# Gate factors moved into ScalarE's copies of transposes, and weight decoding started on another rhythm, in a fused attention and two-layer kernel

## The chip, the cores and the metric

One core of one Trainium2 chip runs the whole kernel in one launch. The metric is the device time of that launch in microseconds (us); smaller is better. Before the change it is 1038.77 us, the median of 3 runs (1038.48 to 1040.22).

## What is computed

`q`, `k`, `v` are 4 batches x 8 heads x 576 positions x 64. Each head gives a causal softmax attention `local` and a memory read `mem_out = (phi(q) @ M) / (phi(q) . z)`, with `phi(x) = max(x,0) + exp(min(x,0))`. The two are mixed per head:

```
g = 1 / (1 + exp(-beta))            # one number per head
x = g * mem_out + (1 - g) * local
```

The 2304 x 512 result goes through two layers of the same form, `g(x @ w_in) @ w_out` with 2048 hidden channels. The first has `g(h) = h - tanh(h)`, the second a ratio of polynomials of `h`. All four weight matrices arrive as 64-bit floats and are turned into two fp32r parts (high and low) on the chip.

## The kernel before, in words

**Order.** Nothing is scheduled by a tool: every engine executes its instructions in the order in which the program issues them. In the attention stage that order is a hand-made table: each of the 16 head pairs has some 60 named events (`AT`, `OVER`), each with a due time, and a heap issues them in order of time. After attention, plain loops give the order.

**Attention, one pair `n` of heads.** `scores` (L857) writes q.k products into PSUM for units `i` = 0 to 4 (unit 4 holds the 64 tail rows of both heads). `least` (L873, VectorE, DVE below) masks them, writes them to SBUF and takes each row's minimum of the negated scores; for unit 4 two partial minima are combined by a 1-column operation (L879). `expo` (L886, ScalarE, ACT below) exponentiates and sums. `recip` (L895, L898, DVE) gives 1/sum. `scale` (L906, GpSimd, POOL below) multiplies each row by 1/sum and by `1 - g` of its head in one instruction with two scalar operands. `turn` (L925) transposes the scaled probabilities on TensorE (PE below) in seven groups (`TURNS`), and `turned` (L938, ACT) copies each group from PSUM to SBUF. `values` (L974) multiplies by v. Beside this, `norm1` (L795, POOL), `norm2` (L804, L805, L807, DVE) and `norm3` (L812, POOL) form phi divided by phi.z and times `g`; the factor `g` is L807. `phiT` (L822, PE) transposes phi and `phiC` (L829, ACT) copies it out; `memory` (L958) adds phi @ M onto the same PSUM bank as the values. `setup2` (L1285 to L1292) computes `g`, `1 - g` and a copy of `1 - g` laid out for unit 4.

**Weight decoding.** A background list of pieces (class `Background`, L623) advances when `tick()` is called. A piece is loaded (L557, L559), and at consecutive ticks gets an ACT step (L575), two DVE operations (L577, L578), two more (L582, L585), and then either a split into high and low (L595, L597) or a store to DRAM (L611) for later. Up to two pieces are under way at once.

**Layer 1** runs in two passes: chunks 0 to 3 of the hidden channels on tiles of 256 tokens, woven into and after attention (first lines L1049, L1078, L1079, L1084, L1085, L1096), and chunks 4 to 15 on six tiles of 384 tokens. The second pass is the loop at L1451 with 72 steps (12 a tile). At each of its steps `bg.tick()` is called once for tile 0 and twice after it (L1463, L1465); in this pass the 32 pieces of layer 2's weights are decoded and stored. **Layer 2** follows (L1131 to L1189).

Of the kernel before, what the change touches and what calls it, by code (L numbers as in the profile page):

```python
# [10 lines left out]
F32 = mybir.dt.float32  # L11
F32R = mybir.dt.float32r
I64 = mybir.dt.int64
U32 = mybir.dt.uint32
AF = mybir.ActivationFunctionType
ALU = mybir.AluOpType
AX = mybir.AxisListType
PSUM = bass.MemoryType.PSUM

P = 128  # L20
# [7 lines left out]
TURNS = (((2, 0, 3), (0, 0, 1)), ((2, 1, 3), (0, 1, 1)), ((3, 0, 4),), ((3, 1, 4),), ((1, 0, 2), (1, 1, 2)), ((4, 0, 4),), ((4, 1, 1),))  # L28
MIX_FROM = 680.0
BG_FROM = 411.57  # L30
N_PT = 6
AGE_A, AGE_B, AGE_C = 1, 3, 4

AT = {'s1': 48.5,
 's2': -9.21,
# [427 lines left out]
BANKS_1 = ([0, 1], [2, 5], [3], [4], [6, 7])  # L463
# [8 lines left out]
def kernel(  # L472
# [19 lines left out]


    nc = tc.nc
    B, NP, _, _, S = qd.shape
    H, D = 2 * NP, mz.shape[2] // 2
    NT, DM = out.shape
# [70 lines left out]
    def w_decode(layer, f, s):  # L568


        words = wraw.pop((layer, f, s)).bitcast(U32).rearrange("p (c t) -> p c t", t=2)
        low, high = words[:, :, 0], words[:, :, 1]
        x = bg.buf("wf", [P, DM], U32, f"wf{layer}_{f}_{s}")
        xf = x.bitcast(F32)
        nc.scalar.activation(xf, high.bitcast(F32), AF.Abs)  # L575
        yield
        nc.vector.tensor_scalar(xf, xf, E_MIN, E_MAX, ALU.max, ALU.min)  # L577
        nc.vector.tensor_scalar(  # L578
            x, x, 5, 2, ALU.logical_shift_left, ALU.logical_shift_right
        )  # L580
        yield
        nc.vector.scalar_tensor_tensor(  # L582
            x, high, 0xC0000000, x, ALU.bitwise_and, ALU.bitwise_or
        )
        nc.vector.scalar_tensor_tensor(  # L585
            x, low, 29, x, ALU.logical_shift_right, ALU.bitwise_or
        )
        yield
        return xf

# [32 lines left out]
    class Background:  # L623
# [3 lines left out]
        def __init__(self):  # L627
            self.q, self.live, self.nl, self.ns, self.held = [], [], 0, 0, 0
            self.ring = {t: [(stage, t)] * 2 for t in ("wraw", "wf")}
            self.at = {"wraw": 0, "wf": 0}  # L630
            self.now, self.loaded, self.age = 0, [], 1

        def more(self, pool):
            for t in self.ring:
# [6 lines left out]

        def leave(self):

            while self.ns - len(self.live) < self.mark:
                self.tick(self.ns < self.mark)

        def buf(self, tag, shape, dt, name):
# [12 lines left out]
        def tick(self, start=True):  # L660
            self.now += 1
            for item in list(self.live):
                item[0] += 1
                self.held -= item[0] == item[1]
                if next(item[3], self) is self:
                    self.live.remove(item)
            if (
                start and self.ns < self.nl
                and self.now >= self.loaded[self.ns] + self.q[self.ns][4]
                and len(self.live) < len(self.ring["wf"])  # L670
            ):
                _, done, key, work, _ = self.q[self.ns]
                self.ns += 1
                next(work)
                self.live.append([1, done, key, work])
            while self.nl < len(self.q) and self.held < len(self.ring["wraw"]):
                load, _, key, *_ = self.q[self.nl]
                load(*key)
                self.held += 1
                self.loaded.append(self.now)  # L680
                self.nl += 1
# [21 lines left out]
    class Attention:  # L703
# [95 lines left out]

        def norm2(self, n):  # L800

            d, h = self.pair[n], 2 * (n % NP)
            nrm = d["nrm"] = self.sp.tile([P, NQ + 1, 2], F32, tag="nrm", name=f"nrm{n}")
            nc.vector.tensor_reduce(nrm, self.cp["pz"][n % 2], AX.X, ALU.add)  # L804
            nc.vector.reciprocal(nrm, nrm)  # L805
            gg = self.cp["g"][:, h:h + 2].unsqueeze(1)
            nc.vector.tensor_tensor(nrm, nrm, gg.to_broadcast([P, NQ + 1, 2]), ALU.mult)  # L807

        def norm3(self, n):
            d = self.pair[n]  # L810
# [15 lines left out]
        def phiC(self, n, k):  # L826
            d = self.pair[n]
            j0, w = ((0, TB), (TB, TAIL))[k]
            nc.scalar.copy(d["phiT"][:, j0:j0 + w], d.pop(("php", k))[:, 0:w])  # L829


        def scores(self, n, units):
# [29 lines left out]
        def least(self, n, i):  # L862

            v, cp = self.u[n, i], self.cp
            sm = v["sm"]
            for c, (bank, c0, k0, k1, _, mask) in enumerate(v.pop("jobs")):
                if i < NQ:
                    v["p"].append(self.sp.tile(
                        [P, k1], F32, tag=f"p{i}_{c}", name=f"p{n}_{i}_{c}", bufs=1
                    ))  # L870
                elif c == 0:
                    v["p"].append(cp["p4"])
                nc.vector.tensor_tensor_reduce(  # L873
                    out=v["p"][-1][:, k0:k1], in0=bank[:, c0:c0 + k1 - k0], in1=mask,
                    scale=-0.125, scalar=3.0e38, op0=ALU.add, op1=ALU.min,
                    accum_out=sm[:, 4 + c:5 + c],
                )
            if i == NQ:
                nc.vector.tensor_tensor(sm[:, 4:5], sm[:, 4:5], sm[:, 5:6], ALU.min)  # L879

        def expo(self, n, i, e):

            v = self.u[n, i]
            sm, pt = v["sm"], v["p"][e]
            pt = pt[:, 0:S] if i == NQ else pt
            nc.scalar.activation(  # L886
                pt, pt, AF.Exp, bias=sm[:, 4 + e:5 + e], scale=-1.0,
                accum_out=sm[:, 2 * e:2 * e + 1],
            )

# [8 lines left out]

        def scale(self, n, i, e):  # L900
            v, h = self.u[n, i], 2 * (n % NP)
            pt = v["p"][e]
            og, c = (self.cp["omg"], h + e) if i < NQ else (self.cp["omg4"], n % NP)
            pt = pt[:, 0:S] if i == NQ else pt
            eng = nc.vector if (n, i, e) == (0, NQ - 1, 0) else nc.gpsimd
            eng.tensor_scalar(  # L906
                pt, pt, v["sm"][:, 6 + e:7 + e], og[:, c:c + 1], ALU.mult, ALU.mult
            )

        def busy(self, ps, count):  # L910

# [19 lines left out]
        def turned(self, n, k):  # L931
            ps = self.pair[n].pop(("tp", k))
            w = sum(nb for _, _, nb in TURNS[k])
            if w == 1:
                t = self.sp.tile([P, 1, P], F32, tag="pT5", name=f"pT{n}_{k}")
            else:
                t = self.sp.tile([P, NQ, P], F32, tag="pT", name=f"pT{n}_{k}", bufs=N_PT)
            nc.scalar.copy(t[:, 0:w, :].rearrange("r t c -> r (t c)"), ps[:, 0:w * P])  # L938
            c = 0
            for i, e, nb in TURNS[k]:  # L940
                self.u[n, i].setdefault("pT", {})[e] = t[:, c:c + nb]
                c += nb
# [303 lines left out]
    cp["g"] = cpool.tile([P, H], F32, tag="gg", name="gg")  # L1246
    cp["omg"] = cpool.tile([P, H], F32, tag="omg", name="omg")
    cp["omg4"] = cpool.tile([P, NP], F32, tag="omg4", name="omg4")
    cp["sm"] = [cpool.tile([P, 8], F32, tag=f"sm{j}", name=f"sm{j}") for j in range(2 * NQ + 2)]
    cp["rq"] = [cpool.tile([P, S + TAIL], F32, tag=f"rq{j}", name=f"rq{j}") for j in range(2)]  # L1250
    cp["mb"] = [cpool.tile([P, P], F32, tag=f"mb{j}", name=f"mb{j}") for j in range(3)]
# [31 lines left out]
    def setup2():  # L1283
        g, omg = cp["g"], cp["omg"]
        nc.scalar.activation(g, g, AF.Exp, scale=-1.0)  # L1285
        nc.vector.tensor_scalar(g, g, 1.0, None, ALU.add)
        nc.vector.reciprocal(g, g)
        nc.vector.tensor_scalar(omg, g, -1.0, 1.0, ALU.mult, ALU.add)
        o2 = omg.rearrange("r (p e) -> r p e", e=2)
        for e in range(2):  # L1290
            r = slice(e * TAIL, (e + 1) * TAIL)
            nc.vector.tensor_copy(cp["omg4"][r], o2[r, :, e])  # L1292

    bS, bT, bV = (Banks(i) for i in BANKS_0)
    bHa, bYa = (Banks(i) for i in BANKS_1[3:])
# [30 lines left out]
    bg.more(wke)  # L1326
    bg.age = AGE_A
    for f in FA:
        bg.add(1, f, w_direct, f"wa{f}", nc.gpsimd)
    for f in FB[len(FB) - KEEP:]:  # L1330
        bg.add(1, f, w_keep)
    attn.start(setup)
# [22 lines left out]

    while events:
        at, _, name, n = heapq.heappop(events)
        if attn.done and not mixed:
            mixed = True
            bS.ids, bT.ids, bV.ids = BANKS_1[:3]  # L1360
        if name in ("h", "xs") and (not mixed or flow["n"] == len(one.items)):
# [38 lines left out]
    slot_of = {f: f"wb{j}" if j < nb else f"wa{j - nb}" for j, f in enumerate(FB)}  # L1400
    for j, f in enumerate(FB):
        if j < len(FB) - KEEP:
            bg.add(1, f, w_direct, slot_of[f], nc.gpsimd)
    bHa.ids = bHa.ids + BANKS_1[0]
    tiles = list(range(NT // TM))
    two = None
    while any(flow["line"]) or one.out or flow["n"] < len(one.items):
        advance(True, True)
        left = len(one.items) - flow["n"]
        if left == LESS_AT:  # L1410
            bg.less()
        if left == 0 and two is None:
            bg.leave()
            wke_ctx.close()
# [36 lines left out]
    for s in range(ni + 2):  # L1451
# [7 lines left out]
        if s < ni:  # L1459
            two.gate1(t, f)  # L1460
            if s % nf in SPLITS_1 and t + 1 < len(tiles):
                xs1.ready(t + 1, SPLITS_1[s % nf])
            bg.tick()  # L1463
            if t > 0:
                bg.tick()  # L1465
        if s >= 2:
            two.tail(*items[s - 2])
# [97 lines left out]
```

## Time and profile before

| | before |
|---|---|
| median of 3 runs | 1038.77 us |
| the profiled execution, its own time | 1039.35 us |
| its span, first to last instruction | 1037.6 us |
| mean granted TensorE clock | 0.996 |
| PE busy, share of the span | 97% |
| DVE, ACT, POOL busy | 76%, 68%, 35% |

All rows below come from that one profiled execution. A span row gives busy time by engine; a chain row follows the work that ended last, back from the end, so that a piece of it is time that nothing else hid. A matmul's end is modelled, and a busy PE is not a PE at its peak. "issue" in the chain is time in which an engine waited for nothing that the profile shows.

### The profile page before, as it was taken

The page shows a single profiled execution, that of the slowest core. Times are in us where ns is not written, and L with a number is a line of the kernel's source. Part 1 is how long each engine was busy: PE and PEld are TensorE (multiplying, and loading weights), DVE is VectorE, ACT ScalarE, POOL GpSimd, SP SyncE. Part 2 cuts the span into 40 slices and gives each one's busy share as a digit, 9 for nine tenths or more (in the row PEclk, how much of TensorE's full clock was granted, in tenths as well). Part 3 has the DMA queues.
Part 4 walks back from the last instruction along what each step waited for, and adds up shares of the span by engine and source line. Part 5 has one row for each costly group of instructions (what it writes and reads, how often), then busy time and mean ns, then how long its engine had stood idle before and what let it go on. Part 6 is the DMA issues. An engine that isn't in the chain of part 4 may idle for free.

```text
span 1037.6 us, 18004 instructions
## 1 busy us (share of the span) xinstructions
PE 1010.9 (97%) x6446; PEld 912.2 (88%) x6446; DVE 784.7 (76%) x1759; ACT 701.5 (68%) x1492; POOL 362.6 (35%) x380
## 2 busy tenths in 40 slices
PE   7999999999988999999999999999999999999998
PEld 4766777888988999999999999999999999999997
DVE  5889999874878366757676767987877877877885
ACT  5878877785555443333333556998888888888886
POOL 4878896673543010101000101332332423323221
PEclk9999999999999999999999999999999999999999
DMA  4445556432232124444444441000000000000000
GB/s 131 124 148 146 166 133 203 140 109 73 82 103 82 41 92 122 122 128 128 136 126 123 141 144 41 21 1 32 1 11 22 1 31 1 1 31 1 22 10 31
DMA packets 37674, 82.97 MB, mean 80 GB/s; under 512 B 8528, under 2 KB 11088, under 8 KB 37584
## 3 DMA queue, kind: packets, MB, share of 16 engines
q1 hardware_dynamic: 37120, 81.55, 26.1%
q8 instruction: 51, 0.84, 0.3%
q14 instruction: 39, 0.32, 0.1%
q10 hardware_dynamic: 464, 0.27, 0.1%
HBM read 66.07 MB, written 15.73 MB: 79 GB/s over the span
## 4 chain that ended last, share of the span: by engine, by line
PE 80%; DVE 12%; ACT 4%; issue 2%; POOL 1%; DMA 0%; SPq 0%; DVEq 0%; ACTq 0%; POOLq 0%
PE h L1049 35%; PE y L1179 19%; PE y L1096 17%; PE s L857 3%; DVE p L873 3%; PE tp L925 2%; PE pv L974 2%; DVE wf L585 2%; DVE wf L582 1%; ACT p L886 1%; DVE gl L1085 1%; DVE wf L577 1%; DVE phi L789 1%; PE pw L974 1%; DVE wf L578 1%
## 5 line engine op out<-in xcount | busy, mean ns | idle before, releaser
L1049 PE MATMUL h<-xs,w 128*128 128x384 f32 (+1 forms) x2448 | 437.4, 327 | 1.6 <-POOL xs L1041 0.7
L1049 PEld LDWEIGHTS h<-xs,w 128*128 128x128 f32 x2448 | 408.2, 188 | 12.5 <-POOL xs L1041 1.3
L1096 PE MATMUL y<-gh,w 128*128 128x384 f32 (+1 forms) x864 | 216.3, 318 | 3.0 <-ACT gh L1084 2.9
L1179 PE MATMUL y<-w,gh 128*128 128x512 f32 x576 | 179.6, 393 | 0.0
L1096 PEld LDWEIGHTS y<-gh,w 128*128 128x128 f32 x864 | 152.2, 189 | 4.3 <-ACT gh L1084 3.1
L1096 PE MATMUL y<-gl,w 128*128 128x384 f32 (+1 forms) x432 | 137.6, 318 | 4.0 <-DVE gl L1085 3.9
L1041 POOL TENSOR_TENSOR xs<-x,xs 128x256 fp32r<-128x256 f32 (+1 forms) x56 | 51.3, 940 | 256.1 <-ACT xs L1040 232.8
L1078 ACT ACTIVATE g<-h 128x384 f32<-128x384 f32 (+1 forms) x108 | 49.2, 455 | 134.6 <-PE h L1049 121.0
L1079 DVE TENSOR_TENSOR g<-h,g 128x384 f32<-128x384 f32 (+1 forms) x108 | 55.2, 512 | 97.2 <-ACT g L1078 97.0
L906 POOL TENSOR_SCALAR p<-p,sm,omg 128x256 f32<-128x256 f32 (+4 forms) x143 | 109.2, 773 | 48.8 <-DVE sm L898 34.7
L1179 PEld LDWEIGHTS y<-w,gh 128*128 128x128 f32 x576 | 106.8, 188 | 17.4
L1179 PE MATMUL y<-w,gl 128*128 128x512 f32 x288 | 114.0, 396 | 0.2
L1168 POOL TENSOR_TENSOR gl<-g,gh 128x384 fp32r<-128x384 f32 x48 | 49.5, 1031 | 149.8 <-ACT gh L1166 149.8
L1168 POOL TENSOR_TENSOR gl<-vG,gh 128x384 fp32r<-128x384 f32 x47 | 50.3, 1070 | 131.2 <-ACT gh L1166 129.0
L886 ACT ACTIVATE p<-p,sm 128x128 f32<-128x128 f32 (+4 forms) x144 | 84.9, 592 | 12.2 <-DVE sm L873 8.3
L1084 ACT CAST gh<-g 128x384 fp32r<-128x384 f32 (+1 forms) x108 | 51.6, 478 | 61.2 <-PE y L1096 58.6
L1096 PEld LDWEIGHTS y<-gl,w 128*128 128x128 f32 x432 | 81.6, 189 | 5.2 <-DVE gl L1085 5.2
L1155 DVE TENSOR_TENSOR vA<-vA,vC 128x384 f32<-128x384 f32 x96 | 53.5, 558 | 42.9 <-ACT vC L1149 42.9
L873 DVE CUSTOM_DVE_ANT_0 p<-s,mask 128x512 f32<-128x512 f32 (+4 forms) x160 | 69.5, 478 | 17.3 <-PE s L857 15.2
L1085 DVE TENSOR_TENSOR gl<-g,gh 128x384 fp32r<-128x384 f32 (+1 forms) x108 | 61.8, 573 | 23.6 <-ACT gh L1084 23.6
L857 PE MATMUL s<-rk,rq 64*128 64x512 f32 (+5 forms) x320 | 71.9, 475 | 7.8 <-DVE sm L873 5.1
L1144 DVE SCALAR_TENSOR_TENSOR vA<-vA,vC 128x384 f32<-128x384 f32 x96 | 59.3, 618 | 25.2 <-ACT vC L1143 20.1
(95 smaller groups left out, 1607.2 us busy)
## 6 DMA issues: line engine op xcount, KB each, us to landing
wraw<-in_w_in_dram SPq DMA_DIRECT2D x32, 512.0 KB, 4.1
wraw<-in_w_out_dram SPq DMA_DIRECT2D x32, 512.0 KB, 4.0
wk<-wf SPq DMA_DIRECT2D x42, 256.0 KB, 4.4
wx<-wk SPq DMA_DIRECT2D x21, 512.0 KB, 3.3
qn<-in_qn_dram SPq DMA_DIRECT2D x16, 320.0 KB, 3.7
vn<-in_vn_dram SPq DMA_DIRECT2D x16, 320.0 KB, 4.3
out_dram<-o SPq DMA_DIRECT2D x18, 256.0 KB, 2.0
rk<-in_kd_dram SPq DMA_DIRECT2D x30, 144.0 KB, 2.8
```

What stands on the lines that cost most here:

```text
L857: nc.tensor.matmul(bank[:, c0:c0 + k1 - k0], d["rq"][r, q0:q0 + P], d["rk"][r, k0:k1], start=True, stop=True, skip_group_check=True,)
L873: nc.vector.tensor_tensor_reduce(out=v["p"][-1][:, k0:k1], in0=bank[:, c0:c0 + k1 - k0], in1=mask, scale=-0.125, scalar=3.0e38, op0=ALU.ad ...
L886: nc.scalar.activation(pt, pt, AF.Exp, bias=sm[:, 4 + e:5 + e], scale=-1.0, accum_out=sm[:, 2 * e:2 * e + 1],)
L906: eng.tensor_scalar(pt, pt, v["sm"][:, 6 + e:7 + e], og[:, c:c + 1], ALU.mult, ALU.mult)
L1049: nc.tensor.matmul(ps[:, 0:T], wi_of(layer, f, wp, k), xs[k][:, xp], start=(n == 0), stop=(n == 3 * NK - 1),)
L1079: nc.vector.tensor_tensor(v["g"], v["h"], v["g"], ALU.subtract)
L1085: self.lo.tensor_tensor(v["gl"], v["g"], v["gh"].bitcast(F32), ALU.subtract)
L1096: nc.tensor.matmul(ps, wo_of(1, f, w)[:, m * P:(m + 1) * P], v[g], start=(first and j == 0 and m % n == 0), stop=(last and j == 2), skip_g ...
L1144: nc.vector.scalar_tensor_tensor(A, A, QEPS, C, ALU.add, ALU.mult)
L1155: nc.vector.tensor_tensor(n["A"], n["A"], n["C"], ALU.mult)
L1168: eng.tensor_tensor(o["gl"], o["G"], o["gh"].bitcast(F32), ALU.subtract)
L1179: nc.tensor.matmul(acc_of[t][m], g[:, c], wo_of(2, f, w), start=(first and j == 0), stop=(last and j == 2),)
```

## The change

1. **Probabilities.** For units 0, 2 and 3 (`LATE`) POOL multiplies by 1/sum alone, one operation with one scalar operand. The factor `1 - g` is applied in `turned`: the ACT copy of that transpose group becomes an activation `Copy` whose scale is a per-partition operand holding the head's `1 - g`. Groups 0 to 3 of the seven hold those units. Units 1 and 4 stay as they were.
2. **Norm.** L807 goes. `phiC` becomes an activation `Copy` with scale `g` (new tile `g4`, laid out by head pair), filled by two more small copies in `setup2`.
3. **Unit 4's minimum.** L879, a `tensor_tensor` of two 1-column operands, becomes a `tensor_reduce` over those two neighbouring columns into column 7, which `expo` then reads.
4. **Decoding.** A layer 2 piece starts only 3 ticks or more after the last start (`EVERY`), and after tile 0 the number of ticks per step follows a 12-entry list (`TICKS_1`, sum 24) where it was 2 at each step.

The event table, its times and the events' names stay. Other new names (`N_P`, `MIX`, `PSUM_DECODE`, `SCALES`, `ENG`, `LOW_*`, `bg.banks`, `bg.inside`) hold values with which the code does what it did: `PSUM_DECODE` is False, and every engine letter is "P".

```diff
+SCALES = "PPPPPPPPP"
+LATE = (0, 2, 3)
+EVERY = 3
+TICKS_1 = (2, 2, 2, 3, 2, 3, 2, 2, 2, 2, 2, 0)
...
             if (
                 start and self.ns < self.nl
                 and self.now >= self.loaded[self.ns] + self.q[self.ns][4]
+                and (self.q[self.ns][2][0] == 1 or self.now >= self.last + EVERY)
                 and len(self.live) < len(self.ring["wf"])
             ):
                 _, done, key, work, _ = self.q[self.ns]
+                self.last = self.now
...
         def norm2(self, n):
...
             nc.vector.reciprocal(nrm, nrm)
-            gg = self.cp["g"][:, h:h + 2].unsqueeze(1)
-            nc.vector.tensor_tensor(nrm, nrm, gg.to_broadcast([P, NQ + 1, 2]), ALU.mult)
...
         def phiC(self, n, k):
-            nc.scalar.copy(d["phiT"][:, j0:j0 + w], d.pop(("php", k))[:, 0:w])
+            nc.scalar.activation(
+                d["phiT"][:, j0:j0 + w], d.pop(("php", k))[:, 0:w], AF.Copy,
+                scale=self.cp["g4"][:, n % NP:n % NP + 1],
+            )
...
             if i == NQ:
-                nc.vector.tensor_tensor(sm[:, 4:5], sm[:, 4:5], sm[:, 5:6], ALU.min)
+                nc.vector.tensor_reduce(sm[:, 7:8], sm[:, 4:6], AX.X, ALU.min)
...
         def scale(self, n, i, e):
-            eng = nc.vector if (n, i, e) == (0, NQ - 1, 0) else nc.gpsimd
-            eng.tensor_scalar(
-                pt, pt, v["sm"][:, 6 + e:7 + e], og[:, c:c + 1], ALU.mult, ALU.mult
-            )
+            how = "V" if (n, i, e) == (0, NQ - 1, 0) else SCALES[2 * i + e]
+            eng = nc.vector if how == "V" else nc.gpsimd
+            if i == NQ:
+                og = self.cp["omg4"][:, n % NP:n % NP + 1]
+                eng.tensor_scalar(pt[:, 0:S], pt[:, 0:S], r, og, ALU.mult, ALU.mult)
+            elif i not in LATE:
+                og = self.cp["omg"][:, h + e:h + e + 1]
+                eng.tensor_scalar(pt, pt, r, og, ALU.mult, ALU.mult)
+            elif how == "A":
+                nc.scalar.activation(pt, pt, AF.Copy, scale=r)
+            else:
+                eng.tensor_scalar(pt, pt, r, None, ALU.mult)
...
-            nc.scalar.copy(t[:, 0:w, :].rearrange("r t c -> r (t c)"), ps[:, 0:w * P])
+            dst, (i, e, _) = t[:, 0:w, :].rearrange("r t c -> r (t c)"), TURNS[k][0]
+            if i in LATE:
+                c = 2 * (n % NP) + e
+                nc.scalar.activation(
+                    dst, ps[:, 0:w * P], AF.Copy, scale=self.cp["omg"][:, c:c + 1]
+                )
+            else:
+                nc.scalar.copy(dst, ps[:, 0:w * P])
...
         for e in range(2):
             r = slice(e * TAIL, (e + 1) * TAIL)
             nc.vector.tensor_copy(cp["omg4"][r], o2[r, :, e])
+            nc.vector.tensor_copy(cp["g4"][r], g2[r, :, e])
...
-            bg.tick()
-            if t > 0:
+            for _ in range(TICKS_1[s % nf] if t else 1):
                 bg.tick()
```

## Rows read from the trace of the kernel before

**Rows 1.** Busy time by engine in six stretches of the span (us; instructions in brackets).
```profile
core 0: us, PE busy (x) PEld busy (x) DVE busy (x) ACT busy (x) POOL busy (x), PEclk, DMA share, GB/s
...
77.00:125.00 48.00, 44.78 (x385) 32.69 (x383) 44.95 (x146) 39.09 (x106) 41.20 (x44) 0.96 0.49 147
125.00:252.00 127.00, 124.52 (x1174) 101.81 (x1174) 102.99 (x348) 95.21 (x265) 87.75 (x98) 1.00 0.48 142
...
345.00:640.00 295.00, 294.74 (x1699) 294.18 (x1698) 193.18 (x332) 122.58 (x240) 26.42 (x24) 1.00 0.40 118
640.00:1037.60 397.60, 393.13 (x1965) 353.79 (x1964) 319.83 (x576) 338.83 (x608) 119.52 (x115) 1.00 0.04 14
```

**Rows 2.** Chain that ended last, 12 to 28 us: start, us, what.
```profile
12.70 0.16 DVE omg L1292
...
12.87 0.17 DVE omg L1292
...
13.62 0.52 POOL p L906
...
14.34 1.61 POOL p L906 x2
...
16.32 0.94 POOL p L906
...
19.92 0.17 DVE nrm L807
...
21.86 2.46 POOL p L906 x3
```

**Rows 3.** The same chain, 66 to 117 us: pieces of L879 and L807.
```profile
67.83 1.39 DVE sm L879
...
87.63 0.04 DVE nrm L807
87.66 0.27 issue
...
94.79 0.43 DVE sm L879
...
116.52 0.04 DVE nrm L807
116.56 0.26 issue
```

**Rows 4.** Small DVE operations by line: duration ns min/median/max, first and last start.
```profile
L879 DVE TENSOR_TENSOR sm<-sm x16: 159/160/1379, 15.4 to 242.4; 128x1 f32<-128x1 f32 x16
...
L895 DVE TENSOR_REDUCE sm<-sm x80: 135/148/159, 13.1 to 245.4; 128x2 f32<-128x4 f32 x64, 128x1 f32<-128x2 f32 x16
```

**Rows 5.** Groups by shape, DVE: busy us, mean ns.
```profile
L879 DVE TENSOR_TENSOR sm<-sm 128x1 f32<-128x1 f32 x16 | 4.7, 293 | 0.6
...
L807 DVE TENSOR_TENSOR nrm<-nrm,gg 128x10 f32<-128x10 f32 x16 | 3.8, 237 | 0.5
```

**Rows 6.** POOL: L906 by line (ns min/median/max), one of it, one without scalar operands.
```profile
L906 POOL TENSOR_SCALAR p<-p,sm,omg x143: 442/768/1432, 13.6 to 246.0; 128x384 f32<-128x384 f32 x32, 128x128 f32<-128x128 f32 x32, 128x256 f32<-128x256 f32 x32, 128x512 f32<-128x512 f32 x31
...
72.42 0.82 POOL L906 TENSOR_SCALAR p<-p,sm,omg 128x576 f32<-128x576 f32 x1 [0.73 <-ACT p L886]
...
L1266 POOL TENSOR_SCALAR_AFFINE_SELECT mask<-mask 128x128 f32<-128x128 f32 x1 | 0.3, 294 | 0.1
```

**Rows 7.** Groups by shape, ACT, PSUM to SBUF: without and with scale and bias operands.
```profile
L1148 ACT ACTIVATE vA<-h 128x384 f32<-128x384 f32 x96 | 46.9, 489 | 39.4 <-PE h L1049 37.4
...
L1152 ACT ACTIVATE vG<-h,coef 128x384 f32<-128x384 f32 x48 | 31.5, 656 | 0.0
```

**Rows 8.** The chain again: first and last ACT copies on it (L829, L938).
```profile
31.66 0.10 ACT phiT L829
...
54.40 0.59 ACT pT L938
...
214.98 0.10 ACT phiT L829
...
219.12 0.49 ACT pT L938
```

**Rows 9.** Who waited for whom, 0 to 250 us: us in total, times, longest.
```profile
ACT pT L938 <- PE tp L925: 18.6, 25, 2.3
...
PEld tp L925 <- POOL p L906: 12.4, 18, 1.6
...
PE tp L925 <- POOL p L906: 2.7, 4, 1.0
```

**Rows 10.** Waits of 345 to 640 us: PE's only one, and ACT's cast behind PE.
```profile
ACT gh L1084 <- PE y L1096: 56.8, 55, 1.6
...
PE h L1049 <- DVE w L621: 0.3, 1, 0.3
```

**Rows 11.** Groups by shape, DVE: the last two operations of a decode step.
```profile
L585 DVE SCALAR_TENSOR_TENSOR wf<-wraw,wf 128x512 uint32<-128x512 uint32 x64 | 52.8, 824 | 2.2
L582 DVE SCALAR_TENSOR_TENSOR wf<-wraw,wf 128x512 uint32<-128x512 uint32 x64 | 51.9, 811 | 0.6
```

More of the change, by code (lines that the diff above doesn't have):

```diff
@@ L31 @@
 N_PT = 6
+N_P = 1
+MIX = True
+PSUM_DECODE = False
+SCALES = "PPPPPPPPP"
+LATE = (0, 2, 3)
+LOW_ATT, LOW_POST, LOW_X = "P", "P", "P"
 AGE_A, AGE_B, AGE_C = 1, 3, 4
+EVERY = 3
+TICKS_1 = (2, 2, 2, 3, 2, 3, 2, 2, 2, 2, 2, 0)
 AT = {'s1': 48.5,
@@ L494 @@
     nc = tc.nc
+    ENG = {"P": nc.gpsimd, "V": nc.vector}
     B, NP, _, _, S = qd.shape
@@ L572, in w_decode @@
         low, high = words[:, :, 0], words[:, :, 1]
-        x = bg.buf("wf", [P, DM], U32, f"wf{layer}_{f}_{s}")
-        xf = x.bitcast(F32)
+        nm = f"wf{layer}_{f}_{s}"
+        if bg.banks:
+            x = bg.banks(nm + "x").bitcast(U32)
+            bg.inside += 1
+        else:
+            x = bg.buf("wf", [P, DM], U32, nm)
+        inside, xf = bool(bg.banks), x.bitcast(F32)
         nc.scalar.activation(xf, high.bitcast(F32), AF.Abs)
@@ L584, in w_decode @@
         )
+        y = bg.buf("wf", [P, DM], U32, nm) if inside else x
         nc.vector.scalar_tensor_tensor(
-            x, low, 29, x, ALU.logical_shift_right, ALU.bitwise_or
+            y, low, 29, x, ALU.logical_shift_right, ALU.bitwise_or
         )
+        bg.inside -= inside
+        xf = y.bitcast(F32)
         yield
@@ L631, in __init__ @@
             self.now, self.loaded, self.age = 0, [], 1
+            self.banks, self.inside, self.last = None, 0, 0
         def more(self, pool):
@@ L642, in leave @@
         def leave(self):
-            while self.ns - len(self.live) < self.mark:
+            while self.ns - len(self.live) < self.mark or self.inside:
                 self.tick(self.ns < self.mark)
@@ L800, in norm2 @@
         def norm2(self, n):
-            d, h = self.pair[n], 2 * (n % NP)
+            d = self.pair[n]
             nrm = d["nrm"] = self.sp.tile([P, NQ + 1, 2], F32, tag="nrm", name=f"nrm{n}")
@@ L868, in least @@
                     v["p"].append(self.sp.tile(
-                        [P, k1], F32, tag=f"p{i}_{c}", name=f"p{n}_{i}_{c}", bufs=1
+                        [P, k1], F32, tag=f"p{i}_{c}", name=f"p{n}_{i}_{c}", bufs=N_P
                     ))
@@ L878, in least @@
             if i == NQ:
-                nc.vector.tensor_tensor(sm[:, 4:5], sm[:, 4:5], sm[:, 5:6], ALU.min)
+                nc.vector.tensor_reduce(sm[:, 7:8], sm[:, 4:6], AX.X, ALU.min)
         def expo(self, n, i, e):
             v = self.u[n, i]
-            sm, pt = v["sm"], v["p"][e]
+            sm, pt, c = v["sm"], v["p"][e], 7 if i == NQ else 4 + e
             pt = pt[:, 0:S] if i == NQ else pt
             nc.scalar.activation(
-                pt, pt, AF.Exp, bias=sm[:, 4 + e:5 + e], scale=-1.0,
+                pt, pt, AF.Exp, bias=sm[:, c:c + 1], scale=-1.0,
                 accum_out=sm[:, 2 * e:2 * e + 1],
@@ L901, in scale @@
             v, h = self.u[n, i], 2 * (n % NP)
-            pt = v["p"][e]
-            og, c = (self.cp["omg"], h + e) if i < NQ else (self.cp["omg4"], n % NP)
-            pt = pt[:, 0:S] if i == NQ else pt
-            eng = nc.vector if (n, i, e) == (0, NQ - 1, 0) else nc.gpsimd
-            eng.tensor_scalar(
-                pt, pt, v["sm"][:, 6 + e:7 + e], og[:, c:c + 1], ALU.mult, ALU.mult
-            )
+            pt, r = v["p"][e], v["sm"][:, 6 + e:7 + e]
+            how = "V" if (n, i, e) == (0, NQ - 1, 0) else SCALES[2 * i + e]
[10 more added lines that the diff above has]
+                eng.tensor_scalar(pt, pt, r, None, ALU.mult)
         def busy(self, ps, count):
@@ L937, in turned @@
                 t = self.sp.tile([P, NQ, P], F32, tag="pT", name=f"pT{n}_{k}", bufs=N_PT)
-            nc.scalar.copy(t[:, 0:w, :].rearrange("r t c -> r (t c)"), ps[:, 0:w * P])
+            dst, (i, e, _) = t[:, 0:w, :].rearrange("r t c -> r (t c)"), TURNS[k][0]
[4 more added lines that the diff above has]
+                )
+            else:
+                nc.scalar.copy(dst, ps[:, 0:w * P])
             c = 0
@@ L1248 @@
     cp["omg4"] = cpool.tile([P, NP], F32, tag="omg4", name="omg4")
+    cp["g4"] = cpool.tile([P, NP], F32, tag="g4", name="g4")
     cp["sm"] = [cpool.tile([P, 8], F32, tag=f"sm{j}", name=f"sm{j}") for j in range(2 * NQ + 2)]
@@ L1288, in setup2 @@
         nc.vector.tensor_scalar(omg, g, -1.0, 1.0, ALU.mult, ALU.add)
-        o2 = omg.rearrange("r (p e) -> r p e", e=2)
+        o2, g2 = (t.rearrange("r (p e) -> r p e", e=2) for t in (omg, g))
         for e in range(2):
@@ L1328 @@
     for f in FA:
-        bg.add(1, f, w_direct, f"wa{f}", nc.gpsimd)
+        bg.add(1, f, w_direct, f"wa{f}", ENG[LOW_ATT])
     for f in FB[len(FB) - KEEP:]:
@@ L1357 @@
         at, _, name, n = heapq.heappop(events)
-        if attn.done and not mixed:
+        if MIX and attn.done and not mixed:
             mixed = True
@@ L1402 @@
         if j < len(FB) - KEEP:
-            bg.add(1, f, w_direct, slot_of[f], nc.gpsimd)
-    bHa.ids = bHa.ids + BANKS_1[0]
+            bg.add(1, f, w_direct, slot_of[f], ENG[LOW_POST])
+    bHa.ids = BANKS_1[3] + BANKS_1[0]
+    if PSUM_DECODE:
+        bg.banks = Banks(BANKS_1[1] + BANKS_1[2])
+    xs_a.eng = ENG[LOW_X]
     tiles = list(range(NT // TM))
@@ L1411 @@
             bg.less()
+        if left <= 2:
+            bg.banks = None
         if left == 0 and two is None:
```

## The prediction

> **What bounds the kernel now.** I read the busy time by stretch first. From 345 us to the end PE is the engine that works without a gap: 294.74 of 295 us, then 393.13 of 397.6 [rows 1]. What can still move lies before that, in attention, where no engine alone sets the pace: from 77 to 125 us DVE is busy 44.95 of 48 us, from 125 to 252 us PE 124.52 of 127 with DVE at 103 and ACT at 95 [rows 1]. So I read the chain that ended last, to see which instructions of this change lie on it. It passes back and forth between PE, DVE and ACT, and touches L807, L879, L906, L829 and L938 in a few places only [rows 2, 3, 8]. Third come the durations of those lines by shape [rows 4 to 7], and last the waits [rows 9, 10].
>
> All engines run in issue order and the order stays, so I count what leaves or joins the chain; time won before 345 us shifts all that follows, since nothing later starts by a clock.
>
> **L879, the unit 4 minimum.** It is on the chain in 7 of 16 pairs, with 0.17, 1.39, 0.20, 0.43, 0.16, 0.16 and 0.16 us, 2.67 in all (the two longest stand in [rows 3]). An undisturbed one takes 159 ns, yet one took 1379 [rows 4]. Its successor is a `tensor_reduce` like L895, which took 135 to 159 ns in all 80 cases among the same neighbours, mean about 148 [rows 4]. 7 x 0.148 = 1.04, so the gain is 1.63 us. The least gain is 7 x 0.012 = 0.08, if whatever held L879 up holds up the next DVE operation instead.
>
> **L807, the factor g in the norm.** It is on the chain in 5 pairs: 0.17 twice in the first pairs [rows 2], 0.04 three times from 87 to 117 us, there followed by 0.27, 0.08 and 0.26 us of "issue" before the next DVE operation starts [rows 3]. Together 0.34 + 0.12 + 0.61 = 1.07 us that go. Without the two long delays (0.27 and 0.26 brought down to 0.08) it is 0.70, the least gain. POOL's norm3 behind it starts earlier; nothing more is counted for that.
>
> **Set-up.** The two L1292 copies are on the chain, 0.16 and 0.17 us [rows 2]. Two more of their kind stand beside them: +0.33 us.
>
> **L906 on POOL, one operand less.** No row shows POOL's single-operand form. The shortest L906, 128 columns, took 442 ns; POOL's pass over 128 columns without scalar operands, the affine select, 294 [rows 6]. Two operands and a second multiply thus cost at most 148 ns, and I take half, 74, for the one that goes; the ends are 0 and 148. Seven L906 lie on the chain, all in the first two pairs [rows 2]: 7 x 0.074 = 0.52 us gained, with ends 0 and 1.04. The other 88 of the 95 POOL instructions in question are hidden: PE waited for L906 in 4 places only, 2.7 us in all, while most of the weight loader's 12.4 us ran beside matmuls [rows 9].
>
> A rule of the Trainium skill speaks against this gain. From 128 columns to 576, L906 goes from 442 to 820 ns, 0.84 ns a column [rows 6]. The GPSIMD Engine Reference, section "Elementwise — side-by-side cycle accounting", says that a loop body of up to two operations is bound by the read and write port at 1.03 cycles an element, 0.86 ns at the 1.2 GHz it gives; the trace agrees. So, by that rule, dropping the second multiply would save nothing per column; by that the sum below would be 1.28 us of gain, and the time 1037.5.
>
> **The scaled ACT copies.** 4 of 7 L938 per pair and both L829 get a scale operand: 64 + 32 = 96 instructions. From PSUM, 128x384 without operands takes 489 ns and with two 656 [rows 7]: (656 - 489) / 2 = 83.5 ns each, some 8.0 us of ACT time. The chain holds 12 pieces of L938, from 54.40 to 219.12 us, and 6 of L829, from 31.66 to 214.98 [rows 8]. 12 x 4/7 is about 7, plus 6 makes 13 x 0.0835 = 1.09 us lost. The ends are 0 (the copy only shortens a wait behind it) and 18 x 0.0835 = 1.50. The rest is covered by ACT's idle time, 32 us from 125 to 252 [rows 1], with ACT itself waiting for the transposes 25 times [rows 9]; if that cover goes, see the second rival.
>
> **Decoding.** I count ticks through the 72 steps of the loop. Before, the 32 layer 2 pieces start at steps 11 to 58; after, at steps 12 to 57, each at most one step away from where it was, eight in a tile both times, and none in a tile's last step. Nothing is left over for the flush at step 60. The DMAs move with them: the last store goes from step 59 to 60, the loads' buffers come free a step earlier at the end, and SP's queue has the same number of entries. In this stretch PE waits once, for 0.3 us, for another line, and ACT's cast waits for PE's matmuls 55 times, not the reverse [rows 10]. So 0, with 0.3 us as the most to win; the price of a collision is the third rival.
>
> **Sum.** -1.63 - 1.07 + 0.33 - 0.52 + 1.09 = -1.80 us, against the profiled execution's own 1039.35: 1037.55. That execution is 0.58 us above the median of 1038.77, so on the median: 1037.0. At the ends: -1.63 - 1.07 + 0.33 - 1.04 = -3.41, 1035.4; and -0.08 - 0.70 + 0.33 + 1.50 = +1.05, 1039.8.
>
> **Rivals.** *DVE's relief counts everywhere.* If DVE's queue set the pace in all 16 pairs, all of L807 (16 x 237 ns = 3.79 us) and the shortening of L879 (16 x 145 = 2.32) would show [rows 5]: -6.11 + 0.33 - 0.52 + 1.09 = -5.21, 1033.6 us. For it: DVE is 94% busy from 77 to 125 us [rows 1], and freed DVE time may also relieve collisions with POOL that I don't see. Against it: the chain holds only 7 and 5 of the 16.
>
> *ACT becomes the bound.* If ACT's copies hold up its exponentials, and these the transposes of the next turn, the whole 8.02 us shows: -1.63 - 1.07 + 0.33 - 0.52 + 8.02 = +5.13, 1043.9 us. It makes the kernel measurably slower once some 60 of the 96 copies are on the path, (2.08 + 2.89) / 0.0835, against 13 now. For it: ACT is 81% busy from 77 to 125 us and the chain passes through it repeatedly up to 219 us. Against it: the idle time above.
>
> *A decode step lands in front of a gate.* L582 and L585 take 0.81 + 0.82 us [rows 11]. If such a pair now stood once per tile in front of a gate that PE needs at once, four tiles would cost 4 x 1.64 = 6.5 us beside the gain: 1043.5 us. DVE's 102 us of idle time in that stretch [rows 1] speak against it.
>
> **How the numbers follow.** The measurement tells 0.2%, 2.08 us, from no change: faster is under 1036.7, slower above 1040.8. My own sum has a chance of 0.58; its ends reach over the line, so 0.16 of that is faster and 0.42 within. Wide DVE relief has 0.24 (faster). ACT as the bound has 0.12 (slower) and decode collisions 0.06, half of it slower, half within. Faster 0.16 + 0.24 = 0.40; within 0.42 + 0.03 = 0.45; slower 0.12 + 0.03 = 0.15. The likeliest is the own sum, 1037.0, alone 1035.4 to 1039.8. The range reaches to the first rival, 1033.6, and a little past it for lucky collisions, 1033.0; at the top past the sum's end to 1040.5, leaving out the two slow rivals and a rest below: 0.2.
>
> **What would show it.** The new minimum at 135 to 160 ns in all 16 cases; L906's 128-column minimum near 368 ns, with units 1 and 4 unchanged; L938 and L829 longer by some 84 ns in the scaled groups; attention ending 1 to 3 us earlier and the same shift standing at 345 us and at the end; PE still without a gap from 345 to 640. Wrong would be: single-operand POOL instructions at the old duration or longer, DVE's long delays moved to its neighbours, ACT without idle time before its exponentials, or any time won or lost after 345 us.

## The result, and the profile after

The changed kernel takes **1051.76 us**, the median of 4 runs (1050.76 to 1052.73), beside 1039.35 us for the kernel before (4 runs, the three of the section above among them). The ratio is 1.0119, 95% interval [1.0102, 1.0137]: 12.4 us slower, where 1.8 us faster was forecast and 1040.5 us was the top of the range.

Where the time went by stretch, as in [rows 1]:

```profile
core 0: us, PE busy (x) PEld busy (x) DVE busy (x) ACT busy (x) POOL busy (x), PEclk, DMA share, GB/s
...
77.00:125.00 48.00, 42.29 (x370) 30.68 (x371) 41.20 (x134) 39.34 (x106) 47.90 (x42) 0.96 0.47 133
125.00:252.00 127.00, 122.00 (x1122) 97.32 (x1121) 108.63 (x351) 96.75 (x259) 112.49 (x101) 1.00 0.45 135
...
345.00:640.00 295.00, 294.74 (x1701) 294.42 (x1700) 187.08 (x329) 119.44 (x239) 25.71 (x25) 1.00 0.40 119
```

From 77 to 125 us POOL is busy 47.90 of 48 us; before it was 41.20, and DVE, then at 44.95, has fallen to 41.20. From 125 to 252 us POOL went from 87.75 to 112.49, though attention no longer ends within this stretch. From 345 to 640 us PE is as full as before, 294.74 us.

The last matmuls of attention, in the timeline of PE, before and then after (start, us):

```profile
252.11 0.80 PE L974 MATMUL pw<-pT,vn 128*64 128x64 f32 x20
```

```profile
264.20 0.80 PE L1008 MATMUL pw<-pT,vn 128*64 128x64 f32 x20
```

Attention ends 12.1 us later. The span grew by 11.7 us (1037.6 to 1049.3), so the whole loss lies in attention and is carried on nearly unchanged. It starts early: the 35th of the 112 copies of transposes comes 7.6 us later already (before, then after):

```profile
78.81 0.57 ACT L938 COPY pT<-tp 128x512 f32<-128x512 f32 x1
```

```profile
86.36 0.57 ACT L972 COPY pT<-tp 128x512 f32<-128x512 f32 x1
```

The instructions that changed, in the changed kernel. L935 is the multiply of units 0, 2 and 3 that was L906 (units 1 and 4 are now L931 and L928); the first two lines are its summary and one of 512 columns, the others groups by shape (count | busy us, mean ns):

```profile
L935 POOL TENSOR_SCALAR p<-p,sm x95: 595/1347/2228, 13.9 to 253.7; 128x384 f32<-128x384 f32 x32, 128x128 f32<-128x128 f32 x32, 128x512 f32<-128x512 f32 x31
...
90.06 1.57 POOL L935 TENSOR_SCALAR p<-p,sm 128x512 f32<-128x512 f32 x1
...
L935 POOL TENSOR_SCALAR p<-p,sm 128x512 f32<-128x512 f32 x31 | 53.7, 1734 | 6.3 <-DVE sm L919 4.3 <-ACT gh L1118 2.0
...
L968 ACT ACTIVATE pT<-tp,omg 128x512 f32<-128x512 f32 x64 | 43.4, 687 | 6.3 <-PE tp L952 6.0
...
L972 ACT COPY pT<-tp 128x512 f32<-128x512 f32 x32 | 18.6, 582 | 15.6 <-PE tp L952 15.6
```

The multiply has one operation less and takes far longer. The shortest, 128 columns, is 595 ns where it was 442 [rows 6]. From 128 to 512 columns it goes to 1.57 us, (1570 - 595) / 384 = 2.5 ns a column, where the rows before gave 0.84. ACT's scaled copies take 687 ns against 582 for the plain ones beside them, 105 ns more where 83.5 was forecast.

The chain that ended last, 83 to 101 us, in the changed kernel:

```profile
83.99 0.60 POOL p L935
...
85.96 1.55 POOL p L935 x2
...
87.75 1.10 POOL p L935
88.85 1.23 POOL w L614
90.08 1.54 POOL p L935
...
93.11 1.75 POOL p L935
94.86 0.04 issue
94.90 0.66 PE tp L952 x4
```

The path runs through POOL's queue: L935, what is queued behind it (L614, a weight split), L935 again, and only then PE's transposes. Before, POOL's multiply of all units stood on the chain with seven instructions, all before 25 us [rows 2]; now L935 alone stands there with 26, in 18 pieces that start from 13.92 to 164.08 us. PE waits for L935 directly, 10 times and 8.6 us in all, where it was 4 times and 2.7 us for all units [rows 9]:

```profile
PE tp L952 <- POOL p L935: 8.6, 10, 2.2
```

### The profile page after: what moved, and what is told of

Read it like the earlier page. It is cut to its first block, busy times and chain, and to the rows that moved or that the text cites. A ratio compares the mean times of both kernels' runs of the same rounds, so it can differ in the third digit from the quotient of the medians.

```text
span 1049.3 us, 17994 instructions
## 1 busy us (share of the span) xinstructions
PE 1014.6 (97%) x6446; PEld 912.8 (87%) x6446; DVE 780.0 (74%) x1745; ACT 709.8 (68%) x1492; POOL 404.4 (39%) x380
## 4 chain that ended last, share of the span: by engine, by line
PE 79%; DVE 10%; POOL 5%; ACT 3%; issue 2%; DMA 0%; SPq 0%; DVEq 0%; POOLq 0%; ACTq 0%
PE h L1083 35%; PE y L1213 19%; PE y L1130 17%; POOL p L935 3%; PE s L878 2%; PE tp L952 2%; DVE p L894 2%; PE pv L1008 1%; DVE wf L600 1%; DVE wf L596 1%; DVE gl L1119 1%; DVE wf L591 1%; POOL xs L1075 1%; ACT p L907 1%; PE pv L992 1%
## 5 line engine op out<-in xcount | busy, mean ns | idle before, releaser
L1075 POOL TENSOR_TENSOR xs<-x,xs 128x256 fp32r<-128x256 f32 (+1 forms) x56 | 49.0, 898 | 258.8 <-ACT xs L1074 235.6
L935 POOL TENSOR_SCALAR p<-p,sm 128x128 f32<-128x128 f32 (+2 forms) x95 | 123.5, 1311 | 23.4 <-ACT p L907 12.0
L952 PEld LDWEIGHTS tp<-ident,p 128*128 128x128 f32 x400 | 46.0, 145 | 38.8 <-POOL p L935 15.2
```

The lines of the kernel that those rows point to most:

```text
L935: eng.tensor_scalar(pt, pt, r, None, ALU.mult)
L952: nc.tensor.transpose(ps[:, (c + j) * P:(c + j + 1) * P], p[:, (c1 + j) * P:(c1 + j + 1) * P], self.cp["ident"],)
L1075: self.eng.tensor_tensor(xs[:, 1], src, xs[:, 0].bitcast(F32), ALU.subtract)
```

## The experiments

**Theory A:** GpSimd runs the multiply without a second operation on a slower path, and that alone makes the kernel slower. **Theory B:** one of the other edits does. Small edits of the multiply, and the decode rhythm, tell them apart.

### e1_imm and e2_ones: the second operation put back

```diff
-                eng.tensor_scalar(pt, pt, r, None, ALU.mult)
+                eng.tensor_scalar(pt, pt, r, 1.0, ALU.mult, ALU.mult)               # e1_imm
+                eng.tensor_scalar(pt, pt, r, self.cp["one"], ALU.mult, ALU.mult)    # e2_ones
```

e2_ones also sets up the tile `one`, 128x1, filled with 1.0 once.

> The changed kernel, but GpSimd's multiply for units 0, 2 and 3 keeps two operations: 1/sum as operand, then the constant 1.0. Theory A (the one-operation form runs slowly on GpSimd: 1552 ns at 512 columns in the trace after, 768 before): its floors return to about 770, 660 and 440 ns for 512, 384 and 128 columns, GpSimd's busy time falls by about 40 us, and the time is 1037 +-2 us, what the other edits were forecast to give. Theory B (the added ScalarE operand, the moved norm factor or the decode rhythm lost the 12 us): the time stays at 1049 to 1053 us, whatever GpSimd does.

> As the run before, but the second operand is a per-partition tile of ones, so that the instruction has the very form of the kernel before. Theory A: 1037 +-2 us and L906's old durations. If only the constant's form is slow: this one is fast and the run before is not. Theory B: 1049 to 1053 us.

Measured: **e1_imm 1034.26 us**, ratio to the kernel before 0.9956 [0.9941, 0.9971]; **e2_ones 1037.39 us**, 0.9987 [0.9978, 0.9996]. L935 by line (ns min/median/max), e1_imm and then e2_ones:

```profile
L935 POOL TENSOR_SCALAR p<-p,sm x95: 360/691/1349, 13.6 to 235.8; 128x384 f32<-128x384 f32 x32, 128x128 f32<-128x128 f32 x32, 128x512 f32<-128x512 f32 x31
```

```profile
L935 POOL TENSOR_SCALAR p<-p,sm,one x95: 438/767/1423, 13.3 to 239.0; 128x384 f32<-128x384 f32 x32, 128x128 f32<-128x128 f32 x32, 128x512 f32<-128x512 f32 x31
```

A multiplication by 1.0 that changes nothing brings the instruction from 595 to 360 ns at the shortest and the kernel from 1051.76 to 1034.26 us, 17.5 us by the medians. (By the ratios to the kernel before, which took 1039.35 us beside the one and 1038.50 beside the other, it is 16.9.) All other edits are still in, so theory B falls. With the operand from memory, 438 ns, the instruction is that of the kernel before (442), and the kernel stands at what the rest of the change is worth. e1_imm came out below the 1037 +-2 expected; its second operand costs 438 - 360 = 78 ns, close to the 74 of the forecast, yet 95 of them are worth 3.1 us, not 0.5.

### e3_before_single: the one-operation form alone

The kernel before, with this in units 0, 2 and 3:

```diff
+            if i in (0, 2, 3):
+                eng.tensor_scalar(pt, pt, r, None, ALU.mult)
```

> The kernel before, with only the one-operation form put into units 0, 2 and 3; the factor 1 - g of those units is left out. Theory A: the whole loss or a little more, 1050 to 1054 us, and 512 columns take 1552 ns at least. Theory B: within 3 us of the kernel before, 1036 to 1042 us.

Measured: 1050.68 us, 1.0115 [1.01, 1.013]. The form alone gives the whole loss. By shape (count | busy us, mean ns):

```profile
L908 POOL TENSOR_SCALAR p<-p,sm 128x512 f32<-128x512 f32 x31 | 53.7, 1734 | 6.4 <-DVE sm L898 4.4 <-ACT gh L1086 2.0
```

### e5_forms: what about the form is slow

```diff
-                eng.tensor_scalar(pt, pt, r, None, ALU.mult)
+                if i == 0:
+                    eng.tensor_scalar(pt, pt, 1.0, None, ALU.mult)
+                elif i == 2:
+                    eng.tensor_scalar(pt, pt, r, 0.0, ALU.mult, ALU.add)
+                else:
+                    eng.tensor_scalar(pt, pt, 1.0, r, ALU.mult, ALU.mult)
```

> Which part of the form is slow on GpSimd. In the changed kernel unit 0 gets one operation with a constant (times 1.0; the 1/sum of that unit is left out), unit 2 gets times 1/sum and plus the constant 0.0, unit 3 gets the constant 1.0 first and 1/sum second. Theory A1 (a missing second operation is slow, whatever its operand): unit 0, 128 columns, stays at 520 ns or more at the floor, 384 and 512 columns are near 580 and 690. Theory A2 (one operand from memory alone is slow, a constant is not): 128 columns near 290 ns. If only multiply-multiply is fast, 384 columns stay at 1237.

Measured: 1034.97 us, a single run. By line (ns min/median/max), units 0, 2 and 3:

```profile
L936 POOL TENSOR_SCALAR p<-p x32: 517/534/1202, 15.6 to 232.5; 128x128 f32<-128x128 f32 x32
...
L938 POOL TENSOR_SCALAR p<-p,sm x32: 574/612/1272, 13.6 to 231.9; 128x384 f32<-128x384 f32 x32
...
L940 POOL TENSOR_SCALAR p<-p,sm x31: 681/692/1332, 14.2 to 236.6; 128x512 f32<-128x512 f32 x31
```

128 columns with one operation take 517 ns even with a constant, nearly as long as 384 columns with two (574). Multiply and add is as fast as multiply twice (574 ns here, 578 in e1_imm, at 384 columns), and the constant first as fast as the operand first (681 and 686 ns at 512). What is slow is the missing second operation, with an operand and, at 128 columns, the one width at which it was tried, with a constant (A1). The operand itself costs 595 - 517 = 78 ns there too.

### e11_unit0 and e12_unit3: the slow form in part

e1_imm, with `eng.tensor_scalar(pt, pt, r, None, ALU.mult)` for `i == 0`, or for `i == 3`, alone.

> The run e1_imm with the one-operation form in unit 0 alone: 32 instructions of 128 columns, each some 235 ns longer at the floor (595 against 360), 7.5 us of GpSimd time. From the runs so far, 3.1 us of span went with 7.6 us of GpSimd time (e2_ones against e1_imm) and 17.5 us with some 72 us by the floors (changed kernel against e1_imm: 32 x 235, 32 x 659 and 31 x 866 ns = 55 us, and longer stalls). Theory (GpSimd's time is on the path with a steady share, 0.3 to 0.4 of it): 1036.5 to 1037.5 us. Rival (only its overflow past a full GpSimd from 77 to 125 us counts): within 0.5 us of e1_imm, 1034 to 1034.9 us.

> The one-operation form in unit 3 alone: 31 instructions of 512 columns, each some 866 ns longer (1552 against 686), 27 us of GpSimd time. Steady share: 1042 to 1045 us. Rival (overflow only): 1037 to 1040 us, since half of GpSimd's added time still finds room in its idle time.

Measured: **1035.23 us**, 0.9965 [0.9952, 0.9978], and **1042.24 us**, 1.0026 [1.0015, 1.0037]. Beside each other, with the busy time of the multiplies of units 0, 2 and 3 summed over the three shapes:

| | POOL, units 0, 2, 3 | time |
|---|---|---|
| e1_imm | 68.7 us | 1034.26 us |
| e11_unit0 | 76.9 | 1035.23 |
| e2_ones | 77.3 | 1037.39 |
| e12_unit3 | 96.4 | 1042.24 |
| the changed kernel | 124.3 | 1051.76 |

Unit 0 lies between the two theories, unit 3 at the lower edge of the steady share. The kernel before took 1039.29 us beside these two and 1038.50 beside e1_imm and e2_ones, so the ratios to it compare better than the times. By them e11_unit0 is not clear of e1_imm (0.9956 [0.9941, 0.9971]): 1.0 of its 8.2 us of added POOL time reaches the end by the medians (0.12), and it may be none. With 27.7 us more in unit 3, 8.0 us reach the end, 7.3 by the ratios (0.26 to 0.29 of it); with 78 ns more in all three units 3.1 of 8.6 us (0.36); with all of it 17.5 of 55.6, 16.9 by the ratios (0.30 to 0.31). A steady share fits three of these and unit 0 badly, so it seems to matter which unit waits; the intervals don't settle it. Whether POOL's time is free up to some threshold stays open. In e12_unit3 POOL is not full on the average from 77 to 125 us, 45.07 of 48, but it is busy all through 84 to 92 us:

```profile
77.00:125.00 48.00, 44.69 (x417) 32.93 (x416) 44.61 (x143) 40.03 (x106) 45.07 (x44) 0.99 0.47 137
...
84.00:92.00 8.00, 6.62 (x56) 4.04 (x52) 7.16 (x26) 6.96 (x21) 8.00 (x8) 1.00 0.35 99
```

### e6_reduce, e7_norm, e8_plain: the other terms one by one

e6_reduce is the kernel before with unit 4's `tensor_reduce`; e7_norm the kernel before without L807, with `scale=g4` in `phiC` and the two set-up copies; e8_plain is e1_imm with the scaled copies plain:

```diff
-            if i in LATE:
+            if False:
...
-            nc.scalar.activation(
-                d["phiT"][:, j0:j0 + w], d.pop(("php", k))[:, 0:w], AF.Copy,
-                scale=self.cp["g4"][:, n % NP:n % NP + 1],
-            )
+            nc.scalar.copy(d["phiT"][:, j0:j0 + w], d.pop(("php", k))[:, 0:w])
```

> The kernel before with the minimum of unit 4 as tensor_reduce alone. The forecast's term: -1.63 us, down to -0.08 if the delays move to the next operation of VectorE. Rival (VectorE's relief counts in all 16 pairs): -2.3 us.

> The kernel before with the factor g moved from the norm into the copy of phi's transpose alone, with the two set-up copies. The forecast's terms: -1.07 (removed) + 0.33 (set-up) + 6 x 0.0835 = 0.50 (copies) = -0.24 us. Rival (relief in all 16 pairs): -3.79 + 0.33 + 0.50 = -2.96 us.

> The run e1_imm (1034.26 us) with all 96 copies plain; the factors 1 - g of units 0, 2 and 3 and g are left out. The forecast's term for the operands is 1.09 us, so 1033.2; if the operands are hidden altogether 1034.3; if all 96 lie on the path (rival of the forecast) 1026.2 us.

Measured: e6_reduce 1037.62 us against 1038.79, 0.9990 [0.9981, 0.9999], so 1.2 us faster. e7_norm 1037.81, 0.9992 [0.9984, 1.0001]: 1.0 us faster by the medians, with an interval that reaches no change. e8_plain 1032.65, 0.9942 [0.9928, 0.9955]: 1.6 us below e1_imm by the medians, with intervals that overlap (e1_imm: [0.9941, 0.9971]). The line of e6_reduce, beside L879 in [rows 4]:

```profile
L879 DVE TENSOR_REDUCE sm<-sm x16: 154/154/156, 15.5 to 240.5; 128x1 f32<-128x2 f32 x16
```

All 16 take 154 to 156 ns, where the `tensor_tensor` of two operands took up to 1379. The delays did not move to DVE's other small operations on the same tile: the longest L895 takes 158 ns and the longest L898 168 in e6_reduce, 159 and 168 in the kernel before.

### e4_old_ticks, e9_imm_ticks, e10_imm_again: the decode rhythm

```diff
-EVERY = 3
+EVERY = 0
...
-            for _ in range(TICKS_1[s % nf] if t else 1):
+            for _ in range(2 if t else 1):
```

e4_old_ticks makes this edit in the changed kernel, e9_imm_ticks in e1_imm; e10_imm_again is e1_imm repeated beside the latter.

> The changed kernel with the old rhythm of decoding: two ticks a step, no minimum distance. Theory A: as the changed kernel, 1050 to 1053 us, and the stretch in which TensorE has no gap as long as before. Theory C (the spread steps land in front of gates): 3 to 7 us faster than the changed kernel.

> The run e1_imm again, as the neighbour of the next one and as the version that is faster than both kernels: 1034.3 +-0.8 us.

> The run e1_imm with the old rhythm of decoding. The forecast put the new rhythm at 0, at most 0.3 us gained: 1034.3 to 1034.6 us, and the stretch of layer 1's second pass as long as with the new rhythm. If the rhythm is worth something: over 1 us more.

Measured: e4_old_ticks 1052.33 us (1051.96 to 1053.42), beside the changed kernel's 1050.76 to 1052.73. e10_imm_again 1034.59 (1034.05 to 1034.75) and e9_imm_ticks 1034.17 (1033.90 to 1034.45), whose ratios 0.9957 [0.9945, 0.997] and 0.9955 [0.9941, 0.9968] can't be told apart. The rhythm is worth nothing that these runs can measure. A stretch of layer 1's second pass, with the new rhythm and with the old:

```profile
344.00:588.00 244.00, 243.74 (x1406) 243.42 (x1406) 158.37 (x281) 92.26 (x184) 21.15 (x21) 1.00 0.40 119
```

```profile
344.00:588.00 244.00, 243.74 (x1406) 243.17 (x1405) 162.23 (x280) 92.90 (x184) 22.96 (x21) 1.00 0.41 119
```

PE is busy 243.74 of 244 us both times. DVE is busy 3.9 us less with the new rhythm, and PE gains nothing by it.

## Why the prediction was wrong, point by point

- **L906 on POOL, one operand less: the step that failed.** "I take half, 74, for the one that goes; the ends are 0 and 148." Neither end was a loss. The step took an instruction with less to do for one that can't take longer, though it said itself that no row shows the single-operand form. The missing row should have opened the range to a loss, with the nearest slower POOL rows as its end. The two things that were bundled in that step come apart in the runs: the operand from memory costs 78 ns at 128 columns (e1_imm against e2_ones), near the 74 taken for operand and multiply together; the missing second operation costs 595 - 360 = 235 ns at 128 columns and 0.88 us at 512 (1.57 us against 0.69 us in e1_imm, below).

```profile
91.60 0.69 POOL L935 TENSOR_SCALAR p<-p,sm 128x512 f32<-128x512 f32 x1
```

- **The rule weighed there.** The Trainium skill's GPSIMD Engine Reference ("Elementwise — side-by-side cycle accounting") says that up to two operations run at the port's 1.03 cycles an element. With two operations the trace agrees (0.84 ns a column). With one it differs, 2.5 ns a column, and the measurement decides. Read as "no gain per column", the rule warned in the right direction and by far too little.
- **How much of POOL lies on the path.** "The other 88 of the 95 POOL instructions in question are hidden." They were not: 95 x 78 ns, the operand alone, are worth 3.1 us (e2_ones against e1_imm), where the forecast had 0.5 for seven on the chain. Of those seven only four belonged to the units that the change touches: the three from 21.86 us on in [rows 2] are one of unit 4 (576 columns) and two of unit 1 (256 columns), which stay, so the step's own sum would have been 4 x 0.074 = 0.30 us. And the time is not paid where the chain had them. The 35th copy of a transpose comes at the same time in e1_imm and e2_ones, at 77 us, and the last matmuls of attention come 3.1 us apart (one execution of each; e1_imm, then e2_ones):

```profile
77.05 0.57 ACT L972 COPY pT<-tp 128x512 f32<-128x512 f32 x1
...
247.25 0.80 PE L1008 MATMUL pw<-pT,vn 128*64 128x64 f32 x20
```

```profile
77.12 0.57 ACT L972 COPY pT<-tp 128x512 f32<-128x512 f32 x1
...
250.35 0.80 PE L1008 MATMUL pw<-pT,vn 128*64 128x64 f32 x20
```

So the pieces of one chain did not tell what a POOL nanosecond is worth: here nothing up to 77 us, where the four lay on it, and all of it later, where none did. That a shortened piece moves the chain on to another queue that runs close behind is a reading that fits and was not shown.

- **L879:** 1.2 us measured, 1.63 forecast, 0.08 at the least. The mechanism held, since the long ones are gone; the difference of 0.4 us is within the interval. **L807 with set-up and phi's copies:** 0.24 forecast, 1.0 measured with an interval that includes both. **The scaled copies:** 1.09 us forecast, 1.6 measured with overlapping intervals, both far from the 8.0 of the rival. One operand was mis-sized, 105 ns measured against 83.5.
- **Together these terms agreed.** e2_ones is the change without any effect on POOL's instruction: -1.63 - 1.07 + 0.33 + 1.09 = -1.28 us forecast, 1037.39 - 1038.50 = -1.1 measured. The intervals of these runs reach some 0.9 us to either side, so the sum is borne out and the size of each part is not.
- **Decoding at 0:** right, by e9_imm_ticks.
- **Rivals.** None happened. The slower side was there as ACT's queue and a decode collision; that the edited instruction itself could get slower was not among them.
- **What would show it.** The forecast's own list named the sign that came: "single-operand POOL instructions at the old duration or longer".

The version that beats both kernels is e1_imm: the change with `1.0` as second factor, 1034.26 us and in the repeat 1034.59, 4.1 to 4.2 us below the kernel before. Which of the decode rhythms it has makes no difference that was measured.

## What to carry to other kernels

An instruction with an operation dropped can be the slower one, here 595 against 360 ns: where the trace has no row of the new form, bound its cost on both sides, or keep the old form by a neutral second operation. In an attention loop in which four engines are over 80% busy (PE, DVE, ACT and POOL from 77 to 125 us [rows 1]), a cost is not free because the chain passes elsewhere today; here some 0.3 of each added microsecond on POOL reached the end in three of four cases, and nothing that was clear of noise in the fourth, unit 0 alone. Check a moved factor by its instruction's duration per column before anything else: here that one line told where the loss came from.

## What was not expected of the hardware

- On GpSimd a `tensor_scalar` with one operation took 595 ns for 128 columns and 1.57 us for 512, with two operations, the second a constant, 360 ns and 0.69 us; the operand from memory added 78 ns at 128 columns in both forms. The same edit made VectorE's one instruction of this line faster: 545 ns with two operands in e2_ones, 486 with one operation in the changed kernel and equally with the constant in e1_imm:

```profile
L935 DVE TENSOR_SCALAR p<-p,sm x1: 486/486/486, 14.1 to 14.1; 128x512 f32<-128x512 f32 x1
```

Why GpSimd's form without a second operation is slow was not tried beyond the forms above.
